# A feed-forward and Fourier-mixing kernel on one core: where ScalarE's long sums of magnitudes may stand among its copies out of PSUM

## The chip, the core and the metric

The kernel runs on one core of a Trainium2 chip. The metric is the device time of one execution in microseconds (us), the median of several runs. TensorE (PE in the profile) multiplies and writes PSUM. ScalarE (ACT) and VectorE (DVE) read PSUM, and every bank that PE fills must be copied or added out by one of them before PE may use it again. GpSimd (POOL) does a maximum across partitions and issues some DMAs. SyncE (SP) issues the others.

## What is computed

```python
x = A_x
xn = _layernorm(x, axis=-1)                      # 2048 x 576
a = einsum("bsd,ed->bse", xn, dft_hid_re)        # Fourier part
b = einsum("bsd,ed->bse", xn, dft_hid_im)
y = einsum("ts,bse->bte", dft_seq_re, a) - einsum("ts,bse->bte", dft_seq_im, b)
h = maximum(einsum("bsd,df->bsf", xn, w1), 0)    # w1: 576 x 4608
return x + y + einsum("bsf,fd->bsd", h, w2)      # w2: 4608 x 576
```

All of it is in float32. The kernel gives TensorE each float32 number as two float16 numbers, a high part and a low part (three products stand for one). For that each block of a weight matrix is first scaled by a power of two that is found from the sums of its magnitudes.

## The kernel before

**Steps.** The 4608 hidden columns are cut into nine blocks of 512 (b = 0 to 8), the 2048 rows into four groups of 512 (g = 0 to 3). A step is one (b, g). For b of 2 and more, 28 steps, both matrix products are done with seven half-size products in place of eight (Strassen's scheme as Winograd has it). This is the stage that the change is about. It starts at 213.6 us and ends at 821.3 us of the profiled span.

**The order of products in a step** is written out by hand (L925 to L932). A step makes the hidden values of its own (b, g) in two pairs of column tiles, `first` and `second`, and multiplies the hidden values of the step before it by w2 (`m`). With P1 and so on for the products of `first`, a prime for those of `second`, and m0 to m6 for the seven products of `mlp2`, PE's order is

P1 P2 m0 P6 P5 m1 P1' P7 m2 P2' P3 P4 m3 P6' m4 P5' m5 P7' m6 P3' P4'

P1, P6 and P7 have 6 matmuls of 256 columns, P2, P3, P4 and P5 have 8, each m has 12 of 288 columns.

**PSUM banks of the pairs** (`pair_products`, L418). P1, P6, P7 and P4 of one pair all add into one bank `u`; P2 has the bank `v`; P5 and then P3 have the bank `w`. Behind most products one instruction takes the bank's running content out (`free`, L465 to L472): ScalarE copies after P1 (L466), P6 (L468) and P5 (L469), VectorE adds after P2 (L467), P7 (L470) and P3 (L471). The next product on the same bank waits for it: P6 for the copy of P1, P7 for the copy of P6, P3 for the copy of P5, P4 for the add of P7. Later ScalarE and VectorE make the two float16 halves of the hidden values: relu copies (L447) with their remainders (L448), a relu on the sum r21 (L476), four sums (L451 to L454), their high half (`end_hi`, L459) and their low half (`end_lo`, L462).

**The seven products with w2** (`mlp2`, L496) go to two PSUM tiles. m0, m2, m3 and m6 are copied out by ScalarE (L519), m1, m4 and m5 are added by VectorE (L521); sums go to DRAM by accumulating DMAs from POOL's queue (`spill`, L523).

**Preparing the next block's weights.** `prepare_block(b + 1)` is a list of small jobs in `todo`; `work()` takes the next one, and a step calls it ten times (the `ready` places of the written order). The jobs are: load w1's two halves (L107), wait some places, sum of magnitudes of a half on ScalarE (`sum_w1`, L581, 1280 elements), power of two from it (POOL's maximum L121, small VectorE instructions), splits into high and low (ScalarE L182, VectorE L183) and sums of blocks (`sums_w1`, L593 to L597), then w2 the same way (load L100, `sum_w2` L610, 1152 elements, splits, `sums_w2` L640 to L643). The pool `raw` has two buffers for the unsplit weights, so a load can start only when the splits of the load two before it are done.

**Magnitudes of the Fourier matrices.** Between the products, `count` (L924) takes the next of 65 passes over them: `sum_c(m - 1)` sums the magnitudes of a tile of 128 x 1024 on ScalarE (L880), then `first_c(m)` loads the next tile (512 KB, L873) into the same single buffer. Every step takes two passes: one after P4, one after m6.

**What fixes the order on an engine.** When the program is built, each engine gets one fixed list. A job that is expected to be ready early may stand ahead of others that come before it in the program. `tc.issue_after(x)` forbids an instruction to stand ahead of x on x's engine. `order["s"]` is the latest `end_hi` (L459), `order["acc"]` the latest L521. `sum_c` may not stand ahead of `order["s"]`. `sum_w1` and `sum_w2` have no such bound.

Of the kernel before, what the change touches and what calls it, by code (L numbers as in the profile page):

```python
# [2 lines left out]

# [10 lines left out]
AF = mybir.ActivationFunctionType  # L14
# [35 lines left out]
def kernel(  # L50
# [364 lines left out]

    banks1, ends = [], []

    def pair_products(b, g, i):  # L418

        if not banks1:  # L420
            banks1.extend(ps1.tile([P, G], F32, tag="ps1", name=f"bank{k}")[:, :GH] for k in range(4))
        h = hs[b, g, i] = mlp.tile([P, 2, 7, GH], F16, tag="h", name=f"h{b}_{g}_{i}", bufs=4)
        st = mlp.tile([P, 5, GH], F32, tag="stage", name=f"s{b}_{g}_{i}")
        r21, s1, s2, s3, s4 = (st[:, n] for n in range(5))
        u, v, w = banks1[i], banks1[2], banks1[3]
        c11, c22 = cbufs[i], cbufs[2]
        tt, stt = nc.vector.tensor_tensor, nc.vector.scalar_tensor_tensor

        def product(n):
            ps = {P2: v, P5: w, P3: w}.get(n, u)  # L430
            first = n in (P1, P2, P5)
            x, ws, a = right(g, n), w1s[b, i], LEFT[n]
            todo = [
                (ws[:, y, a + k], x[z][:, k]) for k in range(2) for y, z in ((1, 0), (0, 0), (0, 1))
            ]
            if n in REST:
                k, c = REST[n]
                todo += [(ws[:, y, k], xT[g][:, KM, (H1, H2)[c]]) for y in range(2)]
            for m, (l, r) in enumerate(todo):
                nc.tensor.matmul(  # L440
                    ps, l, r, start=first and m == 0, stop=m == len(todo) - 1,
                    skip_group_check=not first,
                )

        def value(q, src):
            hi, lo = h[:, 0, q], h[:, 1, q]
            nc.scalar.activation(hi, src, AF.Relu)  # L447
            stt(lo, src, 0.0, hi, ALU.max, ALU.subtract)  # L448

        def end_s():  # L450
            stt(s3, c11, 0.0, r21, ALU.max, ALU.subtract)  # L451
            stt(s1, c22, 0.0, r21, ALU.max, ALU.add)
            stt(s2, c22, 0.0, s3, ALU.max, ALU.subtract)
            stt(s4, u, 0.0, s2, ALU.max, ALU.subtract)  # L454

        hi_s, lo_s = (h[:, k, S1 : S4 + 1] for k in range(2))

        def end_hi():
            order["s"] = nc.scalar.activation(hi_s, st[:, 1:], AF.Copy).ins  # L459

        def end_lo():
            order["lo"] = nc.vector.tensor_tensor(lo_s, st[:, 1:], hi_s, ALU.subtract).ins  # L462


        free = {  # L465
            P1: lambda: nc.scalar.activation(c11, u, AF.Copy),  # L466
            P2: lambda: tt(c11, v, c11, ALU.add),  # L467
            P6: lambda: nc.scalar.activation(s1, u, AF.Copy),  # L468
            P5: lambda: nc.scalar.activation(c22, w, AF.Copy),  # L469
            P7: lambda: tt(c22, u, c22, ALU.add),  # L470
            P3: lambda: tt(r21, w, s1, ALU.add),  # L471
        }  # L472
        use = {
            P2: lambda: value(A11, c11),
            P7: lambda: value(A22, c22),
            P3: lambda: nc.scalar.activation(r21, r21, AF.Relu),  # L476
            P4: lambda: (value(A12, u), end_s(), ends.extend((end_hi, end_lo))),
        }

        def run(n, used=False):  # L480
            if used:
                return use[n]()
            product(n)
            if n in free:
                free[n]()

        return run
# [8 lines left out]
    def mlp2(b, g, n):  # L496
# [19 lines left out]
        o = sums[row, col] = sums[row, col] if b else blocks[:, row, col]  # L516
        if b and n in (0, 2, 3, 6):
            o = sums[row, col] = sumbufs[next(turns) % len(sumbufs)]
            nc.scalar.activation(o, ps, AF.Copy, scale=us[b])  # L519
        else:  # L520
            order["acc"] = nc.vector.scalar_tensor_tensor(o, ps, us[b], o, ALU.mult, ALU.add).ins  # L521
        if b and n not in (0, 2, 3):
# [48 lines left out]
    def sum_w1(b, i):  # L571
# [6 lines left out]
        else:  # L578
            junk = w1bufs[b % 2 * 2 + i].bitcast(F16)
            w1s[b, i] = junk.rearrange("p (n k f) -> p n k f", n=2, f=P)  # L580
        nc.scalar.activation(  # L581
            junk[:, : 2 * KT * P].rearrange("p (k f) -> p k f", f=P), raws["w1", b, i], AF.Abs,
            scale=2.0**-10, accum_out=mx["w1", b][:, i : i + 1],
        )
        if b < BB:
            mx["b", i] = small.tile([P, 1], BF16, tag=f"mb{i}", name=f"mb{b}_{i}")
            nc.vector.tensor_copy(mx["b", i], mx["w1", b][:, i : i + 1])
# [11 lines left out]
    def sum_w2(b, i):  # L599
# [7 lines left out]
        else:  # L607
            new_w2(b, i)
            junk = w2s[b, i][:, 0, :4]
        nc.scalar.activation(  # L610
            junk, raws["w2", b, i], AF.Abs, scale=2.0**-10, accum_out=mx["w2", b][:, i : i + 1]
        )

    def power_w2(b):

# [32 lines left out]
    def split_w2(b, i, c):  # L648
# [4 lines left out]
        q = (slice(B11, B22 + 1), slice(T3, T1 + 1), slice(T4, T2 + 1))[c]  # L653
        split(w[:, 0, q], w[:, 1, q], src, sc["w2", b][:, i : i + 1])

    def prepare_w1(b, i):
        p = power_w1(b, i)
        if b < BB:
# [6 lines left out]
                lambda: split_w1(b, 2 * i + 1),  # L665
            ]
        return [
            lambda: (sum_w1(b, i), next(p)),
            lambda: None,
            lambda: later(p),  # L670
        ], [
# [6 lines left out]

    def prepare_w2(b):
        p = power_w2(b)  # L680
        steps = [
            lambda: sum_w2(b, 0),
            lambda: (sum_w2(b, 1), b > 1 and next(p)),
            lambda: later(p) if b else next(p, None),
        ]
        steps += [lambda i=i: (split_w2(b, i, 0), sums_w2(b, i)) for i in range(NQ)]
        for i in range(NQ):
            steps += [lambda: None] * 2
            steps += [lambda i=i, c=c: split_w2(b, i, c) for c in (1, 2)]
        return steps  # L690

    def prepare_block(b):

        wait = [lambda: None] * (2 if b < BB else 3)
        (m0, s0), (m1, s1) = prepare_w1(b, 0), prepare_w1(b, 1)
        return (
            [lambda: (load_w1(b, 0), load_w1(b, 1))] + wait
            + m0 + s0 + [lambda: load_w2(b, 0)] + m1 + s1 + [lambda: load_w2(b, 1)]
            + wait + prepare_w2(b)
        )  # L700


# [109 lines left out]
    steps = [(b, g) for b in range(NB) for g in range(NG)]  # L812
    todo = []

    def work():
        if todo:
            todo.pop(0)()

    dsp = None

# [54 lines left out]
    def sum_c(m):  # L875

        n, q = divmod(m, 4)
        f = firsts.pop(m)
        with tc.issue_after(order["s"]):
            nc.scalar.activation(  # L880
                f, f, AF.Abs, scale=2.0**-10, accum_out=sums_c[:, n, q : q + 1]
            )
# [5 lines left out]
    for n in range(2, len(steps)):  # L888
# [29 lines left out]
        if b >= BB:  # L918
# [2 lines left out]
            m = lambda q: mlp2(pb, pg, q)  # L921
            end = lambda q: ends and ends.pop(0)()
            ready = lambda q: [work() for _ in range(q)]
            count = lambda q: n > 3 and passes and passes.pop(0)()  # L924
            for do, q in (  # L925
                (first, P1), (first, P2), (m, 0), (end, 0), (first, P6), (ready, 1),
                (first, P5), (later1, P2), (ready, 1), (m, 1), (end, 0), (second, P1), (ready, 1),
                (first, P7), (m, 2), (second, P2), (ready, 1), (first, P3), (first, P4), (count, 0),
                (later1, P7), (m, 3), (second, P6), (later1, P3), (later1, P4), (later2, P2),
                (ready, 1), (m, 4), (second, P5), (ready, 1), (m, 5), (end, 0), (second, P7),  # L930
                (end, 0), (ready, 1), (m, 6), (count, 0), (ready, 2), (second, P3), (second, P4),
                (later2, P7), (later2, P3), (later2, P4), (ready, 1),  # L932
            ):
                do(q)
            for _ in range(4):
# [256 lines left out]
```

## Time and profile before

| | |
|---|---|
| median of 3 runs | 1275.6 us (1275.18 to 1277.2) |
| the profiled execution's own time | 1277.31 us |
| its span, first to last instruction | 1275.5 us |
| stage of the 28 steps | 213.6 to 821.3 us |
| granted TensorE clock | 0.999 |

A row of a timeline gives start, duration, engine, line, operation, out<-in, shapes and count; in brackets how long the engine sat idle before it and what ended that. A row of the waits gives engine and line, what it waited for, and then the idle us in total, how many times, the longest. A row of the windows gives the length of a stretch and each engine's busy us in it. `SPq` is SyncE's queue, where the instruction only issues a DMA; PEld is the weight load beside the matmuls. PE's ends are modelled: a row of 12 matmuls shows 1.63 us although the next product may begin 1.47 us after it.

### The profile page before, as it was taken

How to read it: one execution, taken by the hardware profiler on the slowest of the kernel's cores; microseconds unless marked ns; L12 is line 12 of the kernel's file. 1: busy time of each engine (PE TensorE's matmuls, PEld its weight loads, DVE VectorE, ACT ScalarE, POOL GpSimd, SP SyncE). 2: the span in 40 equal slices, each digit the busy share in tenths (PEclk: the TensorE clock that was granted, in tenths of full speed). 3: DMA queues.
4: the chain of work that ended last, by engine and by line, in shares of the span. 5: the costliest groups of instructions: out<-in, count | busy, mean ns of one | idle time of the engine just before them, and what ended most of it. 6: DMA issues, size and time to landing. Idle time of an engine off the chain costs nothing.

```text
span 1275.5 us, 25491 instructions
## 1 busy us (share of the span) xinstructions
PE 1242.4 (97%) x10396; PEld 987.9 (77%) x10396; DVE 998.6 (78%) x1875; ACT 730.1 (57%) x1222; POOL 149.2 (12%) x188
## 2 busy tenths in 40 slices
PE   8799999999999999999999999999999999999998
PEld 7565566888888878888888888877777777777776
DVE  8989997786887777777868877546788788878875
ACT  5846466676677676776766766534553333333332
POOL 2320011111112121211111111200000000000000
PEclk9999999999999999999999999999999999999999
DMA  6112457566766575665666665630043434434320
GB/s 244 43 66 66 133 123 151 131 115 146 143 129 126 134 146 126 128 144 120 121 145 142 132 136 120 122 96 1 1 161 104 146 116 153 129 117 143 121 85 20
DMA packets 60806, 150.75 MB, mean 118 GB/s; under 512 B 6288, under 2 KB 21136, under 8 KB 60688
## 3 DMA queue, kind: packets, MB, share of 16 engines
q1 hardware_dynamic: 42256, 111.36, 26.9%
q0 software_dynamic: 18432, 37.76, 20.9%
q8 instruction: 81, 1.33, 0.4%
q14 instruction: 37, 0.30, 0.1%
HBM read 101.91 MB, written 47.19 MB: 117 GB/s over the span
## 4 chain that ended last, share of the span: by engine, by line
PE 62%; DVE 20%; DMA 8%; ACT 6%; issue 4%; POOL 1%; SPq 0%; ACTq 0%; POOLq 0%; DVEq 0%
PE p L1126 23%; PE bank L440 15%; PE p L510 15%; PE pd L1008 7%; DMA raw_w<-in_w_dram 3%; DVE w2s L183 2%; DMA f<-in_cre_dram 1%; PE p L310 1%; DVE h L448 1%; ACT f L880 1%; DVE h L462 1%; ACT h L459 1%; DVE acc L521 1%; DMA spill<-sums 1%; DVE h L354 1%
## 5 line engine op out<-in xcount | busy, mean ns | idle before, releaser
L510 PE MATMUL p<-w2s,h 128*128 128x288 f16 x3024 | 409.7, 286 | 4.4 <-DVE acc L521 2.1
L510 PEld LDWEIGHTS <-h 128*128 128x128 f16 x3024 | 295.1, 98 | 81.5 <-issue 6.2
L1126 PE MATMUL p<-R,cs 128*128 128x288 f16 x2688 | 329.8, 286 | 1.7 <-DVE o L1132 1.7
L1126 PEld LDWEIGHTS <-cs 128*128 128x128 f16 x2688 | 263.0, 98 | 68.3 <-issue 2.0
L182 ACT ACTIVATE cs<-c,sc_c 128x1024 f16<-128x1024 f32 x112 | 128.4, 1148 | 193.2 <-PE p L1126 145.6
L440 PEld LDWEIGHTS <-w1buf 128*128 128x128 f16 x1600 | 156.5, 98 | 29.1 <-issue 8.1
L183 DVE SCALAR_TENSOR_TENSOR cs<-c,sc_c,cs 128x1024 f16<-128x1024 f32 x112 | 143.6, 1282 | 40.8 <-ACT cs L182 40.7
L440 PEld LDWEIGHTS <-dbuf 128*128 128x128 f16 x1200 | 117.4, 98 | 21.4 <-issue 5.8
L440 PE MATMUL bank<-xT,w1buf 128*128 128x256 f16 x832 | 109.9, 273 | 2.7 <-ACT acc L469 2.6
L462 DVE TENSOR_TENSOR h<-s,h 128x1024 f16<-128x1024 f32 x56 | 68.5, 1223 | 48.8 <-ACT h L459 48.8
L440 PE MATMUL bank<-acc,w1buf 128*128 128x256 f16 x768 | 102.1, 272 | 2.8 <-DVE acc L470 1.5
L1008 PE MATMUL pd<-dbuf,xT 128*128 128x288 f16 x832 | 104.1, 286 | 0.6 <-DVE R L1037 0.6
L1008 PEld LDWEIGHTS <-xT 128*128 128x128 f16 x832 | 80.7, 98 | 22.9 <-issue 2.9
L523 POOL DMA_DIRECT2D spill<-dbuf x74 | 64.3, 871 | 289.8 <-DVE dbuf L521 223.3
L440 PE MATMUL bank<-xT,dbuf 128*128 128x256 f16 x624 | 82.3, 273 | 1.4 <-ACT acc L469 1.4
L447 ACT ACTIVATE h<-acc 128x256 f16<-128x256 f32 x112 | 46.3, 414 | 58.8 <-DVE acc L470 42.5
L440 PE MATMUL bank<-acc,dbuf 128*128 128x256 f16 x576 | 76.6, 272 | 2.5 <-DVE acc L470 1.1
L1132 DVE SCALAR_TENSOR_TENSOR o<-p,us_c,o 128x288 f32<-128x288 f32 x112 | 57.4, 512 | 20.1 <-PE p L1126 19.5
L448 DVE SCALAR_TENSOR_TENSOR h<-acc,h 128x256 f16<-128x256 f32 x112 | 47.2, 421 | 32.0 <-ACT h L447 31.8
L459 ACT ACTIVATE h<-s 128x1024 f16<-128x1024 f32 x56 | 59.0, 1053 | 22.5 <-DVE s L454 21.3
L880 ACT ACTIVATE f<-f 128x1024 f32<-128x1024 f32 x64 | 67.2, 1050 | 5.4 <-DMA f<-in_cre_dram 5.4
L519 ACT ACTIVATE dbuf<-p,c_ub 128x576 f32<-128x576 f32 x74 | 54.2, 732 | 20.5 <-ACT h L447 11.3
(161 smaller groups left out, 1531.5 us busy)
## 6 DMA issues: line engine op xcount, KB each, us to landing
spill<-dbuf POOLq DMA_DIRECT2D x74, 288.0 KB, 5.1
f<-in_cre_dram SPq DMA_DIRECT2D x32, 512.0 KB, 4.3
f<-in_cim_dram SPq DMA_DIRECT2D x32, 512.0 KB, 3.8
c<-in_cre_dram SPq DMA_DIRECT2D x32, 512.0 KB, 4.5
c<-in_cim_dram SPq DMA_DIRECT2D x32, 512.0 KB, 4.8
spill<-sum POOLq DMA_DIRECT2D x38, 288.0 KB, 5.1
raw_w<-in_w_dram SPq DMA_DIRECT2D x17, 640.0 KB, 5.0
raw_w<-in_w_dram SPq DMA_DIRECT2D x18, 576.0 KB, 3.8
```

Of the source, the lines that this page charges most:

```text
L182: nc.scalar.activation(hi, src, AF.Copy, scale=s)
L183: nc.vector.scalar_tensor_tensor(lo, src, s, hi, ALU.mult, ALU.subtract)
L440: nc.tensor.matmul(ps, l, r, start=first and m == 0, stop=m == len(todo) - 1, skip_group_check=not first,)
L448: stt(lo, src, 0.0, hi, ALU.max, ALU.subtract)
L459: order["s"] = nc.scalar.activation(hi_s, st[:, 1:], AF.Copy).ins
L462: order["lo"] = nc.vector.tensor_tensor(lo_s, st[:, 1:], hi_s, ALU.subtract).ins
L510: nc.tensor.matmul(ps[:, c], h[:, x, qa, c * P : (c + 1) * P], w[:, y, qb], start=first and i == 0 and j == 0, stop=i == NQ - 1 and j == 2 ...
L523: nc.gpsimd.dma_start(spill[g, row, col], o, accum_op=ALU.add)
L880: nc.scalar.activation(f, f, AF.Abs, scale=2.0**-10, accum_out=sums_c[:, n, q : q + 1])
L1008: nc.tensor.matmul(ps[j], xT[g][:, kx, c * P : (c + 1) * P], dsp[j][:, hl, k], start=(t % 2 == 0 and n == 0), stop=(t % 2 == 1 and n == le ...
L1126: nc.tensor.matmul(ps, w[:, a, k], r[:, c, rq], start=first and k == 0 and j == 0, stop=k == HK - 1 and j == 2, skip_group_check=not first,)
L1132: nc.vector.scalar_tensor_tensor(o, ps, us["c"][:, n : n + 1], o, ALU.mult, ALU.add)
```

## The change

Four things are changed. `order["free"]` now holds the latest ScalarE copy out of PSUM (L466, L468, L469, L519), and every long sum on ScalarE may not stand ahead of it (w1's from block 3 on, w2's from block 2 on, and `sum_c`). The sums of w1 and w2 are marked `long`, and seven of the ten places are `brief` (the three that stay `ready` are those before m1, behind P1' and behind P2'): there a long job is not taken but owed, and the next `ready` place takes one job more. The first `count` of a step moves from behind P4 to behind P5'. The empty places among the jobs are redistributed: five in place of three before w1's first sum, one in place of three before w2's, one more between w2's two sums, one fewer before each half's last splits.

```diff
+    def freed(i):
+        order["free"] = i.ins
...
-            P1: lambda: nc.scalar.activation(c11, u, AF.Copy),
+            P1: lambda: freed(nc.scalar.activation(c11, u, AF.Copy)),
-            P6: lambda: nc.scalar.activation(s1, u, AF.Copy),
-            P5: lambda: nc.scalar.activation(c22, w, AF.Copy),
+            P6: lambda: freed(nc.scalar.activation(s1, u, AF.Copy)),
+            P5: lambda: freed(nc.scalar.activation(c22, w, AF.Copy)),
...
-            nc.scalar.activation(o, ps, AF.Copy, scale=us[b])
+            freed(nc.scalar.activation(o, ps, AF.Copy, scale=us[b]))
...
+        with tc.issue_after(order["free" if b > BB else "s"]):
             nc.scalar.activation(
                 junk[:, : 2 * KT * P].rearrange("p (k f) -> p k f", f=P), raws["w1", b, i], AF.Abs,
...
+        with tc.issue_after(order["free"]) if b >= BB else nullcontext():
             nc.scalar.activation(
                 junk, raws["w2", b, i], AF.Abs, scale=2.0**-10, accum_out=mx["w2", b][:, i : i + 1]
...
+    def long(f):
+        f.long = True
+        return f
...
-            lambda: (sum_w1(b, i), next(p)),
+            long(lambda: (sum_w1(b, i), next(p))),
...
-            lambda: sum_w2(b, 0),
-            lambda: (sum_w2(b, 1), b > 1 and next(p)),
+        steps = [long(lambda: sum_w2(b, 0))] + [lambda: None] * (b >= BB)
+        steps += [
+            long(lambda: (sum_w2(b, 1), b > 1 and next(p))),
...
-            steps += [lambda: None] * 2
+            steps += [lambda: None] * (1 if b >= BB else 2)
...
-        wait = [lambda: None] * (2 if b < BB else 3)
+        wait, wait2 = ([lambda: None] * n for n in ((2, 2) if b < BB else (5, 1)))
...
-    def work():
-        if todo:
-            todo.pop(0)()
+    owed = []
+    def work(short=False):
+        if not todo:
+            return
+        if short and getattr(todo[0], "long", False):
+            owed.append(1)
+            return
+        todo.pop(0)()
+        if not short and owed:
+            owed.pop()
+            work(True)
...
-        with tc.issue_after(order["s"]):
+        with tc.issue_after(order.get("free", order["s"])):
             nc.scalar.activation(
                 f, f, AF.Abs, scale=2.0**-10, accum_out=sums_c[:, n, q : q + 1]
...
+            brief = lambda q: [work(True) for _ in range(q)]
...
-                (first, P1), (first, P2), (m, 0), (end, 0), (first, P6), (ready, 1),
+                (first, P1), (first, P2), (m, 0), (end, 0), (first, P6), (brief, 1),
                 (first, P5), (later1, P2), (ready, 1), (m, 1), (end, 0), (second, P1), (ready, 1),
-                (first, P7), (m, 2), (second, P2), (ready, 1), (first, P3), (first, P4), (count, 0),
+                (first, P7), (m, 2), (second, P2), (ready, 1), (first, P3), (first, P4),
                 (later1, P7), (m, 3), (second, P6), (later1, P3), (later1, P4), (later2, P2),
-                (ready, 1), (m, 4), (second, P5), (ready, 1), (m, 5), (end, 0), (second, P7),
-                (end, 0), (ready, 1), (m, 6), (count, 0), (ready, 2), (second, P3), (second, P4),
-                (later2, P7), (later2, P3), (later2, P4), (ready, 1),
+                (brief, 1), (m, 4), (second, P5), (count, 0), (brief, 1), (m, 5), (end, 0), (second, P7),
+                (end, 0), (brief, 1), (m, 6), (count, 0), (brief, 2), (second, P3), (second, P4),
+                (later2, P7), (later2, P3), (later2, P4), (brief, 1),
```

## The prediction

> **What bounds the kernel.** I read in this order: the page's busy times, the windows of single steps, PE's waits in the stage of the 28 steps, and the timelines of one long and one clean step.
>
> ```profile
> PE 1242.4 (97%) x10396; PEld 987.9 (77%) x10396; DVE 998.6 (78%) x1875; ACT 730.1 (57%) x1222; POOL 149.2 (12%) x188
> ...
> 213.60:821.30 607.70, 598.20 (x5155) 503.95 (x5153) 457.06 (x1002) 417.90 (x808) 106.63 (x134) 1.00 0.63 133
> ...
> 387.24:408.45 21.21, 21.21 (x187) 18.00 (x184) 13.89 (x31) 14.31 (x30) 4.25 (x6) 1.00 0.62 130
> 408.45:429.66 21.21, 21.21 (x187) 18.01 (x185) 16.89 (x39) 14.21 (x28) 3.03 (x4) 1.00 0.61 132
> 429.66:450.86 21.20, 21.20 (x186) 18.00 (x184) 15.86 (x40) 15.46 (x31) 4.35 (x6) 1.00 0.66 136
> 450.86:474.06 23.20, 21.84 (x187) 17.97 (x185) 19.17 (x40) 16.97 (x32) 3.32 (x5) 1.00 0.62 131
> 474.06:496.45 22.39, 21.36 (x186) 17.99 (x184) 13.87 (x31) 14.30 (x30) 4.28 (x6) 1.00 0.62 124
> ```
>
> PE is busy 97% of the span, so only its waits can be won. A window row has length, then busy PE, PEld, DVE, ACT, POOL. Steps (4,0) to (4,2) take 21.21 us with PE never idle; (4,3) takes 2.00 more and (5,0) 1.19 more. 28 clean steps would be 28 x 21.21 = 593.9 us; the stage takes 607.7. So 13.8 us is the ceiling of any gain here.
>
> ```profile
> PE bank L440 <- ACT acc L469: 3.9, 5, 0.9
> PE bank L440 <- DVE acc L470: 2.6, 7, 0.4
> PE bank L440 <- ACT s L468: 1.0, 1, 1.0
> ```
>
> The largest wait is for ScalarE's copy of P5 (L469), five times. This is how one comes about, at the end of (4,3):
>
> ```profile
> 468.50 1.27 ACT L581 ACTIVATE w1buf<-raw_w 128x1280 f16<-128x1280 f32 x1 [2.67 <-DMA raw_w<-in_w_dram]
> 469.66 1.63 PE L510 MATMUL p<-w2s,h 128*128 128x288 f16 x12
> 469.77 1.04 ACT L459 ACTIVATE h<-s 128x1024 f16<-128x1024 f32 x1
> 470.72 1.04 ACT L880 ACTIVATE f<-f 128x1024 f32<-128x1024 f32 x1
> 471.76 0.36 ACT L469 ACTIVATE acc<-bank 128x256 f32<-128x256 f32 x1
> 472.17 1.03 PE L440 MATMUL bank<-xT,w1buf 128*128 128x256 f16 x8 [0.88 <-ACT acc L469]
> 473.19 0.81 PE L440 MATMUL bank<-acc,w1buf 128*128 128x256 f16 x6
> ```
>
> w1's sum (L581) stands in ScalarE's list before the copy of P5' and waits 2.67 us for its load. Then come the sum, a 1.04 us high half, a 1.04 us sum of the Fourier tile, and only then the copy that P3' waits for. The clean end of a step, and the start of the next:
>
> ```profile
> 514.44 1.63 PE L510 MATMUL p<-w2s,h 128*128 128x288 f16 x12
> 515.91 1.04 PE L440 MATMUL bank<-xT,dbuf 128*128 128x256 f16 x8
> 516.79 0.82 PE L440 MATMUL bank<-acc,dbuf 128*128 128x256 f16 x6
> 518.90 0.40 ACT L476 ACTIVATE s<-s 128x256 f32<-128x256 f32 x1
> 519.19 1.63 PE L510 MATMUL p<-w2s,h 128*128 128x288 f16 x12
> 519.20 0.36 ACT L447 ACTIVATE h<-bank 128x256 f16<-128x256 f32 x1
> 519.47 0.37 ACT L466 ACTIVATE acc<-bank 128x256 f32<-128x256 f32 x1
> 520.66 0.60 PE L440 MATMUL bank<-acc,dbuf 128*128 128x256 f16 x4
> ```
>
> m6 to P3' is 1.47, P3' to P4' 0.88: 0.109 a matmul of 256 columns. P1 and P2 (14 matmuls, 1.53) end at m0, so this step began at 517.66, and P6 starts 3.00 after a step's start. I use these offsets below.
>
> **The change part by part.** The sum is made against the profiled execution's 1277.31 us (span 1275.5 and 1.8 around it), which is 1.7 above the median of the runs shown, 1275.6.
>
> *1. w1's sums bound to the latest copy.* I counted the jobs through the places: the first half's sum now comes behind the copy of P5 in step (b,1), a whole step after its load, the second half's in (b,2). P1' is the next product that ScalarE copies, m1 and P1' later (1.47 + 0.65 = 2.1 us), longer than the sum (1.27 and its 0.19 of reading), and P6' needs that copy only six products on. Cost 0. If this cover went, P1' would be copied up to 1.5 us late, still ahead of P6'. What goes is the wait above: m6 to P3' was 2.51 against 1.47, then P3' to P4' 1.02 against 0.88, in all 1.18 with 0.88 of it idle in the row. The five waits have 3.9 idle, so 3.9 x 1.18 / 0.88 = **-5.2 us**.
>
> *2. The other long step, (5,0).*
>
> ```profile
> ACT sum L519 <- DMA spill<-sum: 2.3, 1, 2.3
> ```
>
> Its 1.19 us is the wait for L468 in PE's list. ScalarE was held by a copy that waited 2.3 us for an accumulating DMA, right behind the traffic of (4,3)'s end. Between 0 and -1.2; I take the middle, **-0.6**, because the transfers, not the sum, decide it.
>
> *3. The two passes over the Fourier matrices.* The work stays (64 sums, 64 loads), but pass one moves behind the copy of P5' and pass two is bound behind the copy of m6. Before, both were bound only to `end_hi`:
>
> ```profile
> 511.45 0.82 PE L440 MATMUL bank<-acc,dbuf 128*128 128x256 f16 x6
> 511.60 1.05 ACT L880 ACTIVATE f<-f 128x1024 f32<-128x1024 f32 x1
> 512.32 1.63 PE L510 MATMUL p<-w2s,h 128*128 128x288 f16 x12
> 512.76 0.33 SPq L873 DMA_DIRECT2D f<-in_cre_dram  x1
> ```
>
> P5' starts 15.00 us into the step (511.45 - 496.45) and ends at 15.87. Its copy starts 0.2 later and holds ScalarE for 0.3, so the sum of pass one starts at 16.3. The next load is issued 1.16 after a sum's start (511.60 to 512.76): 17.5. m6 ends at 19.46 and its copy at about 20.3. There pass two's sum stands, 2.8 us after its own load was issued.
>
> ```profile
> DMA to landing us min/median/max: 3.5/4.0/8.4
> ...
> DMA to landing us min/median/max: 5.4/5.4/5.4
> ```
>
> The first row is all loads of L873. So ScalarE will wait there in every step: an undisturbed load lands at 21.1 to 21.5. Behind this sum stand the relu on r21, the relu of P4' and the copy of P1, which P6 of the next step needs at 21.21 + 3.00 = 24.21. From the sum's start to the next ScalarE instruction is 1.04 (470.72 to 471.76), then 0.30 and 0.27 (518.90, 519.20, 519.47) and the copy's 0.37: 2.0 us. An undisturbed load costs nothing: 21.5 + 0.1 + 2.0 = 23.6, with 0.6 to spare. That cover is the three products P3' P4' P1 and P2 with m0.
>
> It is gone when another load runs beside. The second row of the fence is the one load issued at 503.89:
>
> ```profile
> 494.29 0.81 ACT L182 ACTIVATE w1buf<-raw_w,c_sw 128x640 f16<-128x640 f32 x1
> ...
> 503.20 0.33 SPq L100 DMA_DIRECT2D raw_w<-in_w_dram  x1
> 503.89 0.33 SPq L873 DMA_DIRECT2D f<-in_cim_dram  x1
> ```
>
> w2's load (L100) starts when the last split of a w1 half is done, 8.9 us after the first split (494.29 to 503.20). In the new order the first split comes about 8.0 us into steps (b,1) and (b,2): P5 ends at 4.53, then copy, sum, maximum, scale (an estimate from the durations above, with 1.6 us for maximum and scale). 8.0 + 8.9 = 16.9, just ahead of the Fourier load at 17.5, as in these rows. Then it lands after 5.4, at 22.9, and the copy of P1 is done at 22.9 + 0.1 + 2.0 = 25.0, 0.8 late. P6 waits; behind the sum the r21 chain is late as well, which m2 needs only at 28.5. That is two steps in each of six blocks: 12 x 0.8 = **+9.6 us**. Bounds: 0, if the list puts the copy of P1 ahead of the sum or the load lands in time; 12 x 1.4 = 16.8, if pass one's sum comes 0.6 later behind a split.
>
> Does the list really put the sum ahead of a copy that could go first? It did so before:
>
> ```profile
> 217.81 6.38 SPq L873 DMA_DIRECT2D f<-in_cre_dram  x2
> ...
> 222.68 1.06 ACT L880 ACTIVATE f<-f 128x1024 f32<-128x1024 f32 x1 [3.30 <-DMA f<-in_cre_dram]
> ```
>
> This sum stood first for 3.30 us while its load was under way. The list counts on earlier landings than the chip gives, as with L581.
>
> A rule of the Trainium skill speaks against this edit: DMA: Bandwidth & Descriptors, section "Rules for kernel authors", says to issue a DMA early and wait on its semaphore late. By it the halved distance between load and sum is a loss. The same page, section "Anatomy of one DMA — SWDGE (gpsimd) path", has a fit of 2.0 us plus bytes at 436 KB a us for another way of issue; as an estimate, 512 KB would land after 3.2 us and this term would be 0, the first rival below. The trace's shortest is 3.5 us and its loaded one 5.4, so the trace does not agree with the fit.
>
> *4. w2's sums and splits later.* Before, w2's sums stood at the end of (b,2), and the splits ran through the first 16 us of (b,3):
>
> ```profile
> 450.74 1.02 ACT L182 ACTIVATE w2s<-raw_w,c_sw 128x864 f16<-128x864 f32 x1 [0.68 <-DVE c_sw L632]
> ...
> 466.19 0.81 DVE L183 SCALAR_TENSOR_TENSOR w2s<-raw_w,c_sw,w2s 128x576 f16<-128x576 f32 x1
> ```
>
> Now the sums come behind the copies of P5 and P1' in (b,3), and the splits start some 11 us later, running into (b+1,0). DVE has 19.17 us of work in (4,3) against 13.87 in (5,0). The crowded stretch cost (4,3) 2.00 - 1.18 = 0.82, mostly P4 behind L470. In its new place it meets P4' behind L470', whose slack is m6 and P3' (2.35 us) in place of m2, P2' and P3 (3.2 us). Bounds: 6 x -0.82 = -4.9 if nothing waits any more; if every wait grows by the 0.85 of lost slack, 6 x 0.85 = +5.1. DVE's load splits over two steps, which helps; the slack is smaller, which hurts. I take **+0.6**.
>
> *5. The rest.* `sum_w2`'s own durations, the empty places, the places of block 1 and the last block's order lie beside a busy PE: 0.
>
> Sum: -5.2 - 0.6 + 9.6 + 0.6 = +4.4 us; 1277.31 + 4.4 = 1281.7 for a profiled execution, less 1.7: **1280.0 us**.
>
> **The rivals.** *Sums that never reach PE* (faster): pass two's sum is followed by the copy of P1 in time, because the list has r21's relu, P4''s relu or that copy ahead of it, or the loads land 0.8 us earlier. For it: undisturbed loads have 0.6 us of slack; w2's load may start after the Fourier load. Against: the rows at 217.81 and 503.20. Then -5.2 - 0.6 + 0.6 = -5.2: 1270.4. It decides at a landing 22.1 us into the step.
>
> *Half of it*: the copy of P1 is late in 12 steps by 0.4 only. -5.8 + 4.8 + 0.6 = -0.4: 1275.2, no change that a measurement can tell.
>
> *The crowded stretch takes over* (slower): P4' waits the full 0.85 more in six steps, and with late splits ahead of the copy of P1 also 0.5 there: 6 x 1.35 = 8.1 in place of 0.6, so 1287.5. For it: DVE's 19.17 us. Against: its work now lies over two steps.
>
> That the change doesn't do what it says: the second sum of w2 stands two products before a copy, m2's, not more; but m2's copy is needed five products later, so this costs nothing and changes no case.
>
> **How the numbers follow.** Late load 0.42, sums that never reach PE 0.36, half of it 0.13, crowded stretch 0.09. The likeliest is the first, 1280.0, with a range of its own of 1277 to 1286. 0.2% is 2.6 us, about what can be told from no change. Faster 0.36, same 0.14, slower 0.50. The range that leaves out 2 in 10 goes from 1267, a little under the faster rival (w2's waits half gone), to 1288.
>
> **What would show it.** Right: L581 never waits for raw_w, PE's five waits for L469 are gone, (b,3) ends without them; L880 waits for DMA some 25 times, about 1 us each; PE waits for L466 at P6 of (b,2) and (b,3), 12 times, about 0.8 us. Wrong: L880 after m6 but no wait of PE for L466; L880 waiting for nothing; or PE's waits for L470 gone from (b,3) without a like wait at P4'.

## The result, and the profile after

The changed kernel takes 1358.31 us (1356.73 to 1361.7, 5 runs) against 1275.6 us for the kernel before in the same session: a ratio of 1.065, 95% interval 1.0631 to 1.0668. It is 82.7 us slower. The prediction was 1280.0, with a range up to 1288. All profiles below number lines as the changed kernel or the experiment does: L444 is the pairs' matmul, L514 the matmul with w2, L470, L472 and L473 ScalarE's copies after P1, P6 and P5, L474 and L475 VectorE's adds after P7 and P3 (L475 makes r21), L480 the relu on r21, L463 `end_hi`, L455 to L458 the four sums ahead of it, L523 ScalarE's copies and L525 VectorE's adds out of the banks of `mlp2`, L527 their accumulating DMA, L182 and L183 the splits, L646 to L649 w2's sums of blocks, L901 the passes' sum, L894 its load.

From the page of the changed kernel (its profiled execution took 1361.7 us): the busy times, the group of the passes' sums with its idle time, and three rows of DMA landings.

```profile
PE 1263.2 (93%) x10396; PEld 994.6 (73%) x10396; DVE 999.0 (73%) x1875; ACT 726.3 (53%) x1222; POOL 147.7 (11%) x188
...
L901 ACT ACTIVATE f<-f 128x1024 f32<-128x1024 f32 x64 | 67.3, 1051 | 88.9 <-DMA f<-in_cre_dram 47.0
...
spill<-dbuf POOLq DMA_DIRECT2D x74, 288.0 KB, 6.9
f<-in_cre_dram SPq DMA_DIRECT2D x32, 512.0 KB, 5.1
f<-in_cim_dram SPq DMA_DIRECT2D x32, 512.0 KB, 5.1
```

The 64 sums are as long as before (67.3 us in all), but ScalarE now stands idle for 88.9 us in front of them. PE is busy for 1263.2 us instead of 1242.4 with the same 10396 instructions, so its matmuls themselves have become longer somewhere. The windows of the four steps (5,0) to (5,3), and of the whole stage, in the columns of the windows before:

```profile
509.36:532.45 23.09, 21.74 (x186) 17.82 (x184) 13.36 (x27) 11.83 (x24) 3.47 (x5) 1.00 0.64 154
532.45:554.57 22.12, 21.53 (x186) 17.98 (x184) 16.19 (x37) 15.12 (x30) 3.30 (x5) 1.00 0.52 108
554.57:581.27 26.70, 22.95 (x187) 18.74 (x184) 16.74 (x38) 15.35 (x31) 4.32 (x6) 0.94 0.55 118
581.27:609.70 28.43, 23.16 (x187) 18.71 (x185) 19.13 (x45) 18.04 (x34) 3.85 (x6) 0.94 0.50 94
212.77:904.24 691.47, 621.19 (x5154) 511.64 (x5152) 456.27 (x1002) 414.85 (x807) 106.12 (x135) 0.97 0.54 115
```

The stage of the 28 steps grew from 607.70 to 691.47 us, by 83.8: all of the loss is here. It has two parts. PE's idle time went from 607.70 - 598.20 = 9.5 to 691.47 - 621.19 = 70.3 us (+60.8), and PE's busy time for the same matmuls by 621.19 - 598.20 = 23.0 us. The steps (b,2) and (b,3) carry most of it, 5.5 and 7.2 us more than the clean 21.21, and just there the granted clock (third number from the right) is 0.94 instead of 1.00.

What PE and ScalarE wait for in the stage, first PE, then ScalarE:

```profile
PE bank L444 <- ACT acc L470: 46.1, 20, 4.5
PE bank L444 <- DVE s L475: 13.3, 6, 2.7
```

```profile
ACT f L901 <- DMA f<-in_cre_dram: 47.0, 14, 5.6
...
ACT f L901 <- DMA f<-in_cim_dram: 39.4, 13, 5.1
```

27 of the sums wait for their load, 3.2 us each on average; PE waits 20 times for the copy of P1 that stands behind such a sum, and six times, once in each (b,3), for the r21 add. The waits for the copy of P5 are gone. This is how a wait for the copy of P1 comes about, at the end of step (5,1), which begins at 532.45 (timeline of the changed kernel):

```profile
548.12 0.82 PE L444 MATMUL bank<-acc,dbuf 128*128 128x256 f16 x6
...
549.95 1.06 ACT L463 ACTIVATE h<-s 128x1024 f16<-128x1024 f32 x1 [0.83 <-DVE s L458]
...
550.65 0.33 SPq L100 DMA_DIRECT2D raw_w<-in_w_dram  x1
550.92 0.36 ACT L473 ACTIVATE acc<-bank 128x256 f32<-128x256 f32 x1
551.18 1.05 ACT L901 ACTIVATE f<-f 128x1024 f32<-128x1024 f32 x1
...
551.61 0.86 POOL L527 DMA_DIRECT2D spill<-sum  x1 [8.91 <-DVE sum L525]
...
552.34 0.33 SPq L894 DMA_DIRECT2D f<-in_cim_dram  x1
...
553.46 0.86 POOL L527 DMA_DIRECT2D spill<-dbuf  x1 [0.99 <-DVE dbuf L525]
...
554.87 0.86 POOL L527 DMA_DIRECT2D spill<-dbuf  x1 [0.55 <-ACT dbuf L523]
...
559.44 1.06 ACT L901 ACTIVATE f<-f 128x1024 f32<-128x1024 f32 x1 [4.87 <-DMA f<-in_cim_dram]
...
561.07 0.37 ACT L470 ACTIVATE acc<-bank 128x256 f32<-128x256 f32 x1
...
561.49 2.72 PE L444 MATMUL bank<-acc,dbuf 128*128 128x256 f16 x12 [3.75 <-ACT acc L470]
```

Read it from the top. P5' is issued from 548.12 on. Its copy (L473) runs only at 550.92, because `end_hi` (L463) stands ahead of it in ScalarE's list and waits for a VectorE sum. The first pass follows at 551.18 and its load goes out at 552.34, 19.9 us into the step, 1.7 us behind w2's load (L100) and with three accumulating transfers (L527) issued around it. The second pass is ready to run and waits 4.87 us, to 559.44, for this load, 7.1 us after its issue. Behind it the copy of P1 ends at 561.44, and P6, whose place in a clean step is 3.00 us after the step's start, so 557.57, starts at 561.49. Then its matmuls and the next product's come 12 in 2.72 us, 0.22 apart instead of the 0.109 of a clean step: after this idle time TensorE runs at half its rate.

### The profile page after: what moved, and what is told of

Its sections match the earlier page's. It is cut to its first block, busy times and chain, and to the rows that moved or that the text cites. A ratio compares the mean times of both kernels' runs of the same rounds, so it can differ in the third digit from the quotient of the medians.

```text
span 1359.9 us, 25517 instructions
## 1 busy us (share of the span) xinstructions
PE 1263.2 (93%) x10396; PEld 994.6 (73%) x10396; DVE 999.0 (73%) x1875; ACT 726.3 (53%) x1222; POOL 147.7 (11%) x188
## 4 chain that ended last, share of the span: by engine, by line
PE 51%; DVE 17%; DMA 13%; ACT 12%; issue 5%; POOL 1%; SPq 0%; ACTq 0%; POOLq 0%; DVEq 0%
PE p L1148 23%; PE p L514 9%; PE pd L1030 8%; PE bank L444 7%; DMA f<-in_cre_dram 6%; DMA f<-in_cim_dram 5%; ACT f L901 4%; PE p L310 3%; DVE h L452 1%; DVE dbuf L183 1%; ACT h L463 1%; DVE w1buf L183 1%; DVE w2s L183 1%; ACT acc L473 1%; DVE h L466 1%
## 5 line engine op out<-in xcount | busy, mean ns | idle before, releaser
L514 PE MATMUL p<-w2s,h 128*128 128x288 f16 x3024 | 420.6, 290 | 13.3 <-DVE h L466 3.2
L514 PEld LDWEIGHTS <-h 128*128 128x128 f16 x3024 | 298.1, 99 | 99.3 <-issue 11.2
L182 ACT ACTIVATE cs<-c,sc_c 128x1024 f16<-128x1024 f32 x112 | 128.4, 1148 | 194.1 <-PE p L1148 150.4
L444 PEld LDWEIGHTS <-w1buf 128*128 128x128 f16 x1600 | 158.8, 99 | 59.4 <-issue 36.1
L183 DVE SCALAR_TENSOR_TENSOR cs<-c,sc_c,cs 128x1024 f16<-128x1024 f32 x112 | 143.6, 1283 | 42.1 <-ACT cs L182 41.9
L444 PEld LDWEIGHTS <-dbuf 128*128 128x128 f16 x1200 | 119.6, 100 | 51.4 <-issue 33.5
L444 PE MATMUL bank<-acc,w1buf 128*128 128x256 f16 x768 | 106.8, 281 | 31.8 <-ACT acc L470 23.5
L901 ACT ACTIVATE f<-f 128x1024 f32<-128x1024 f32 x64 | 67.3, 1051 | 88.9 <-DMA f<-in_cre_dram 47.0
L444 PE MATMUL bank<-xT,w1buf 128*128 128x256 f16 x832 | 110.7, 274 | 0.8 <-DVE s L458 0.8
L455 DVE SCALAR_TENSOR_TENSOR s<-acc,s 128x256 f32<-128x256 f32 x56 | 23.7, 422 | 115.8 <-ACT s L480 115.8
L444 PE MATMUL bank<-acc,dbuf 128*128 128x256 f16 x576 | 80.9, 283 | 29.6 <-ACT acc L470 22.5
L527 POOL DMA_DIRECT2D spill<-dbuf x74 | 64.1, 866 | 296.8 <-DVE dbuf L525 271.5
L451 ACT ACTIVATE h<-acc 128x256 f16<-128x256 f32 x112 | 46.1, 412 | 82.4 <-DVE acc L471 43.6
L466 DVE TENSOR_TENSOR h<-s,h 128x1024 f16<-128x1024 f32 x56 | 68.5, 1223 | 23.6 <-ACT h L463 23.6
L444 PE MATMUL bank<-xT,dbuf 128*128 128x256 f16 x624 | 83.6, 275 | 1.3 <-DVE s L458 1.3
L1154 DVE SCALAR_TENSOR_TENSOR o<-p,us_c,o 128x288 f32<-128x288 f32 x112 | 57.5, 513 | 20.1 <-PE p L1148 19.9
L463 ACT ACTIVATE h<-s 128x1024 f16<-128x1024 f32 x56 | 59.1, 1056 | 15.3 <-DVE s L458 14.4
```

The costliest lines, as they stand in the source:

```text
L182: nc.scalar.activation(hi, src, AF.Copy, scale=s)
L183: nc.vector.scalar_tensor_tensor(lo, src, s, hi, ALU.mult, ALU.subtract)
L444: nc.tensor.matmul(ps, l, r, start=first and m == 0, stop=m == len(todo) - 1, skip_group_check=not first,)
L514: nc.tensor.matmul(ps[:, c], h[:, x, qa, c * P : (c + 1) * P], w[:, y, qb], start=first and i == 0 and j == 0, stop=i == NQ - 1 and j == 2 ...
L527: nc.gpsimd.dma_start(spill[g, row, col], o, accum_op=ALU.add)
L901: nc.scalar.activation(f, f, AF.Abs, scale=2.0**-10, accum_out=sums_c[:, n, q : q + 1])
```

## The experiments

All compare with the kernel before on the same chip, 1276.4 to 1277.5 us there.

| run | what it is | us | ratio, interval |
|---|---|---|---|
| e1 | changed, first pass back behind P4 | 1274.27 | 0.9973, 0.9963 to 0.9983 |
| e2 | before, with the passes' edits alone | 1339.07 | 1.0479, 1.0428 to 1.053 |
| e3 | changed, without the loads | 1275.93 | 0.999, 0.9978 to 1.0002 |
| e4 | before, with the bounds of w1's and w2's sums alone | 1272.86 | 0.9965, 0.9951 to 0.9978 |
| e5 | before, with the first pass's place alone | 1276.71 | 0.9994, 0.9983 to 1.0006 |
| e6 | before, with the passes' bound alone | 1272.63 | 0.9967, 0.9958 to 0.9977 |
| e7 | changed, half of each load | 1332.58 | 1.0437, 1.0414 to 1.046 |
| e8 | before, with all bounds | 1273.04 | 0.9969, 0.9957 to 0.998 |
| e9 | changed, second pass behind the next m1 | 1307.05 | 1.0224, 1.0188 to 1.0261 |
| e10 | passes as in e9, weights as before | 1285.38 | 1.0063, 1.0047 to 1.0078 |
| e11 | all bounds and the first pass's place | 1335.83 | 1.0458, 1.0432 to 1.0483 |
| e12 | changed, one job place later | 1355.24 | 1.0615, 1.0597 to 1.0632 |

The theories on trial first: A, the second pass stands too close behind its own load; B, the moved weight jobs crowd ScalarE and VectorE. **Which half of the change does it?**

```diff
-                (first, P7), (m, 2), (second, P2), (ready, 1), (first, P3), (first, P4),
+                (first, P7), (m, 2), (second, P2), (ready, 1), (first, P3), (first, P4), (count, 0),
...
-                (brief, 1), (m, 4), (second, P5), (count, 0), (brief, 1), (m, 5), (end, 0), (second, P7),
+                (brief, 1), (m, 4), (second, P5), (brief, 1), (m, 5), (end, 0), (second, P7),
```

> The changed kernel, but the first of the two passes over the Fourier matrices is back behind P4; every bound and every job of the weights stays as changed. Theory A (the second pass's sum stands 2.8 us behind its own load and holds ScalarE until it lands, so the copy of P1 and then P6 are late): PE's waits for L470 go, from 46 us to under 3, and with them the slow clock; what stays is P5' behind L475 in (b,3), about 13 us and its echo, so 1280 to 1295 us. Theory B (the moved jobs of the weights are what costs): stays above 1340 us.

The passes' edits alone, on the kernel before:

```diff
-        with tc.issue_after(order["s"]):
+        with tc.issue_after(order.get("free", order["s"])):
...
-                (first, P7), (m, 2), (second, P2), (ready, 1), (first, P3), (first, P4), (count, 0),
+                (first, P7), (m, 2), (second, P2), (ready, 1), (first, P3), (first, P4),
...
-                (ready, 1), (m, 4), (second, P5), (ready, 1), (m, 5), (end, 0), (second, P7),
+                (ready, 1), (m, 4), (second, P5), (count, 0), (ready, 1), (m, 5), (end, 0), (second, P7),
```

> The kernel before, with only the two edits on the passes: the first moved behind P5', both sums bound behind the latest copy out of PSUM. The jobs of the weights are as before. Theory A: most of the loss is here alone, 1310 to 1350 us, L880's line waits for its DMA in nearly every step. Theory B: within 6 us of 1275.6.

One place undone brings 84 us back and leaves the kernel a little faster than before; the passes' edits alone cost 62. e1 is faster than was expected: the waits for r21, which were to stay, are gone as well. PE's waits in e2 are those of the changed kernel without the ones for r21:

```profile
PE bank L444 <- ACT acc L470: 54.9, 27, 5.4
```

**Is it the sum's place on ScalarE, or its load?** e3 keeps the changed kernel's whole order and loads only the first of the 64 tiles.

```diff
         n, q = divmod(m, 4)
-        f = firsts[m] = mlp.tile([P, HK, P], F32, tag="first", name=f"f{n}_{q}", bufs=1)
+        if m:
+            firsts[m] = firsts["kept"]
+            return
+        f = firsts[m] = firsts["kept"] = mlp.tile([P, HK, P], F32, tag="first", name=f"f{n}_{q}", bufs=1)
```

> The changed kernel, but only the first of the 64 loads of Fourier tiles in the passes is done; each pass sums that tile again, with scale 1 in place of 2^-10, so the scales of the Fourier part are not the reference's and 63 loads of 512 KB are left out. ScalarE's instructions and their order of issue bounds are the same. Theory A (the load is what is late, not the 1.24 us of the sum in that place): PE's waits for L470 under 2 us, 1275 to 1295 us. Theory B: above 1340 us. A third way, that the sum's own time in that place is what makes the copy of P1 late: above 1300 us with waits for L470.

```profile
PE bank L444 <- DVE s L475: 8.1, 6, 1.4
...
PE bank L444 <- ACT acc L470: 0.3, 1, 0.3
```

All 64 sums run, 1.05 us each, where the change puts them, and 46.1 us of waiting for the copy of P1 are 0.3. So the sums' length and place cost nothing by themselves: the late load does. The waits for r21 stay, at 1.35 us each instead of 2.2, so the moved jobs cost next to nothing where no load runs beside them.

**The bounds of the weights' sums alone** (e4: `issue_after(order["free"])` around `sum_w1` and `sum_w2` as in the change's diff, nothing else of it).

> The kernel before, with only the bounds on the sums of w1 and w2 (not ahead of the latest copy out of PSUM); places, passes and their bound as before. Theory A with the first term of the prediction: the five waits for L469 at the end of (b,3) go, 1268 to 1272 us. Theory B: no gain or slower, 1275 us or more.

```profile
PE bank L444 <- ACT s L472: 2.8, 7, 0.8
...
PE bank L444 <- ACT acc L473: 0.5, 1, 0.5
```

The waits for the copy of P5 went from 3.9 us in five to 0.5 in one; those for the copy of P6 grew from 1.0 us in one to 2.8 in seven. The median fell by 4.5 us, a little less than expected. In the traces the stage, from the first to the last matmul of the pairs, is 2.9 us shorter (214.6 to 819.3 in place of 213.6 to 821.2). So the first term of the sum is there, but not all of the 4.5 us need belong to it.

**Place or bound?** e5 has only the place of the first `count` changed (the second and third hunk of e2's diff), e6 only the bound (its first hunk).

> The kernel before, with only the place of the first pass moved from behind P4 to behind P5' (the bound stays the last end_hi copy). Theory A (late load): what counts is how much of ScalarE's work lies between a pass's own load and its next sum. The bound to end_hi lets both sums stand where they stood, some ten ScalarE instructions apart, so this costs nothing: 1274 to 1281 us, no wait of a sum for a DMA over 1 us. Rival P (the place alone does it, because the load is issued later): 1320 to 1345 us, as the two edits together had.

> The kernel before, with only the bound of the passes' sums changed to the last copy that frees PSUM; the passes stay behind P4 and behind m6. Theory A: the sums stand eleven to sixteen ScalarE instructions apart, 7 us and more, so a load of 5 to 8 us is nearly always there: 1272 to 1281 us, waits of the sums for DMA under 10 us in total. Rival B (the bound alone does it): 1320 to 1345 us.

Neither costs anything; e6 is even 0.33% faster. The waits for the copy of P5 are gone in e6 too, although its weights' sums have no bound, so they do not need e4's bound to go. With the old bound, the list lets the sum stand at its old position wherever the program has it: e5's order on ScalarE around the sums is that of before, with nine or more instructions between a first sum and the second nearly everywhere. With the old place, the bound leaves ten or eleven between them (e6). Only place and bound together leave few: four or two in e2, two in the changed kernel and five in (b,3). The load of the second sum is issued when the first is done. In e6 these loads land after 5.0 and 5.6 us in the median, no sooner than in the changed kernel, and no sum waits for one: what counts is the distance.

**Does the landing follow the load's bytes?**

```diff
-        f = firsts[m] = mlp.tile([P, HK, P], F32, tag="first", name=f"f{n}_{q}", bufs=1)
-        nc.sync.dma_start(f, blocks_c(n)[q])
+        if not m:
+            firsts["kept"] = mlp.tile([P, HK, P], F32, tag="first", name=f"f{n}_{q}", bufs=1)
+        f = firsts[m] = firsts["kept"]
+        k = HK if not m else HK // 2
+        nc.sync.dma_start(f[:, :k], blocks_c(n)[q][:, :k])
```

> The changed kernel, but every load of the Fourier part after the first brings only half of the tile (256 KB instead of 512 KB; the sum still runs over the whole tile, so the scales of that part differ). Theory A with the landing growing with its bytes: loads land in 2.8 to 4.5 us instead of 5.1 to 7.8, the second sum waits 0.5 to 2.5 us less than before in each step, the waits of P6 fall from 46 us to 5 to 20, TensorE's idle times stay under 3.5 us so that its slow stretches vanish: 1285 to 1315 us. Rival D (the landing is set by a fixed delay or by the queue, not by bytes): landing median stays above 4.8 us and the time above 1340 us.

The landings (page of e7) and the waits for the copy of P1:

```profile
f<-in_cim_dram SPq DMA_DIRECT2D x32, 256.0 KB, 4.2
f<-in_cre_dram SPq DMA_DIRECT2D x31, 256.0 KB, 4.4
```

```profile
PE bank L444 <- ACT acc L470: 30.8, 16, 3.0
```

Both expectations of the time missed. Half the bytes save only 0.7 to 0.9 us of 5.1, and the time falls by 25.7 us, 0.92 us for each of the 28 steps. So the chain holds (what the load gains, the step gains), but most of a landing here isn't its own bytes. The Trainium skill, page "DMA: Bandwidth & Descriptors", section "Queues, rings and completion order", says that a DMA engine takes turns between the queues that have work for it, packet by packet. e10's rows below agree in that other transfers stretch with it; no run here shows the turns themselves.

**Spread the two passes.** e9 leaves the first behind P5' and puts the second behind the next step's m1; e10 does the same on the kernel before with the passes' bound, without the weights' edits.

```diff
-                (first, P5), (later1, P2), (ready, 1), (m, 1), (end, 0), (second, P1), (ready, 1),
+                (first, P5), (later1, P2), (ready, 1), (m, 1), (count, 0), (end, 0), (second, P1), (ready, 1),
...
-                (end, 0), (brief, 1), (m, 6), (count, 0), (brief, 2), (second, P3), (second, P4),
+                (end, 0), (brief, 1), (m, 6), (brief, 2), (second, P3), (second, P4),
```

> The changed kernel with the first pass left behind P5' and the second moved from behind m6 to behind m1 of the next step. Everything else as changed. Theory A: load and sum are eleven ScalarE instructions apart, 7 us or more, so nearly nothing waits: 1270 to 1282 us, waits of the sums for DMA under 12 us in total (the loads beside the weights' load, 6.4 to 7.8 us, are the ones that may still be late). Rival E (a long sum right behind the copy of P5' is itself late for P1's copy, whatever the load does): P1's copy late by about 1 us in 24 steps, 1295 to 1310 us.

> The kernel before with the passes' bound, the first pass behind P5' as in the change, and the second behind m1 of the next step; the weights' sums and jobs as before. Theory A: of the 30 us that the same spread left with all of the change, nearly all lies in (b,3), where the moved w2 jobs stand ahead of the r21 add. With w2 as before it is gone: 1272 to 1283 us, and no wait of PE for that add over 1 us. Rival S (the first load, issued just then, holds up the partial outputs' transfers and so their buffers): 1290 to 1307 us whatever w2 does, with ScalarE waiting 30 us or more for those transfers.

e9's time falls into rival E's range, yet not for its reason: no wait for the copy of P1 is left. Its waits, and one of them at the start of (5,3):

```profile
PE bank L444 <- DVE s L475: 15.5, 6, 2.6
PE bank L444 <- ACT s L472: 8.1, 8, 1.7
```

```profile
557.50 0.74 ACT L523 ACTIVATE sum<-p,c_ub 128x576 f32<-128x576 f32 x1 [3.12 <-DMA spill<-sum]
...
558.56 0.81 PE L444 MATMUL bank<-acc,dbuf 128*128 128x256 f16 x6 [1.30 <-ACT s L472]
```

e10 tells the two apart: without the weights' edits 21.7 us go, with them the r21 waits (0.9 us are left), and 8 us over the kernel before remain. These are ScalarE's waits for accumulating transfers, first e10's waits, then the landings on the pages of e10, e6 and e3:

```profile
ACT dbuf L523 <- DMA spill<-dbuf: 15.5, 13, 2.5
...
ACT sum L523 <- DMA spill<-sum: 12.4, 8, 2.9
```

```profile
spill<-dbuf POOLq DMA_DIRECT2D x74, 288.0 KB, 6.4
```

```profile
spill<-dbuf POOLq DMA_DIRECT2D x74, 288.0 KB, 4.6
```

```profile
spill<-dbuf POOLq DMA_DIRECT2D x74, 288.0 KB, 4.7
```

e6 has the same bound and the same 64 loads, at other moments, and its transfers land as fast as with no loads at all (e3). A load that goes out behind P5' runs into the partial outputs and stretches them to 6.4 us. Both theories were partly right: neither 1283 at most nor 1290 at least.

**The bounds together, and the weights' moves.** e8 adds the bounds of e4 and e6; e11 adds the first pass's place to e8, so it is the change without its moved jobs.

> The kernel before with all of the change's new bounds (sums of the passes, of w1 and of w2) and none of its moves. Theory A: each bound alone gave 4 to 5 us, mostly from the same few waits of PE for the copy of P5; sums and loads stay eleven or more ScalarE instructions apart, so nothing is late: 1268 to 1274 us. Rival: two bounds push each other's sums ahead of P1's copy, 1276 to 1290 us.

> The changed kernel without its second idea: all bounds and the first pass behind P5', but the places of the w1 and w2 jobs as before (no brief, no longer waits ahead of the w2 splits). Theory A: the late second load costs what it cost with the passes' edits alone, and the 19 us between that run and the full change come from the moved w2 jobs: 1330 to 1345 us. Rival B (the sums' bounds cost the 19 us): 1350 to 1362 us.

The two gains don't add up: e4, e6 and e8 all stand at 0.997, and so does e1. No version here is better than that. e11's 1335.83 puts the moved jobs at 22.5 us of the change's 82.7; e9 against e10 gave 21.7. Both pairs have the loads behind P5'. Without loads (e3), and with the pass behind P4 (e1), the same moved jobs cost nothing, so this price needs both.

**Why do they cost that?** In (5,3) of the changed kernel four pairs of w2's block sums and two splits stand ahead of the r21 add on VectorE, and P5' waits:

```profile
598.92 0.82 DVE L646 TENSOR_TENSOR raw_w<-raw_w 128x288 f32<-128x288 f32 x2
...
601.87 0.42 DVE L475 TENSOR_TENSOR s<-bank,s 128x256 f32<-128x256 f32 x1
...
602.34 1.44 PE L444 MATMUL bank<-acc,dbuf 128*128 128x256 f16 x6 [2.60 <-DVE s L475]
```

In e1, with the same moved jobs but the pass behind P4, the add stands ahead of them all, and this wait doesn't occur:

```profile
547.09 0.42 DVE L475 TENSOR_TENSOR s<-bank,s 128x256 f32<-128x256 f32 x1
...
548.06 2.15 DVE L183 SCALAR_TENSOR_TENSOR w2s<-raw_w,c_sw,w2s 128x864 f16<-128x864 f32 x2 [0.54 <-ACT w2s L182]
...
550.12 0.82 DVE L646 TENSOR_TENSOR raw_w<-raw_w 128x288 f32<-128x288 f32 x2
```

e12 moves the place of these jobs behind the products that fill r21:

```diff
-                (first, P7), (m, 2), (second, P2), (ready, 1), (first, P3), (first, P4),
+                (first, P7), (m, 2), (second, P2), (first, P3), (first, P4), (ready, 1),
```

> The changed kernel with one place for a weight job moved from behind P2' to behind P4. Theory L: in (b,3) both first splits of w2 with their eight sums of blocks (L646 to L649) stand ahead of the r21 add (L475) in VectorE's list, and the product P5' waits for that add; behind P4 the add stands ahead of them. Then the six waits for L475 (13.3 us) and the slow matmuls behind them go, some 15 to 22 us: 1332 to 1345 us, with the waits for the copy of P1 as before. Rival (VectorE has too much work in (b,3), whatever its order): the time stays above 1350 us and another wait of 10 us or more stands in (b,3).

```profile
PE bank L444 <- ACT acc L470: 46.5, 26, 4.2
PE bank L444 <- ACT acc L473: 9.2, 6, 2.1
```

My theory missed. The waits for the add are gone, but six waits for the copy of P5 took their place, and the median is only 3 us lower; the intervals of the two ratios (1.0597 to 1.0632 and 1.0631 to 1.0668) touch. The rival, too much work in (b,3) whatever its order, had the time right and its wait nearly: 10 us or more were expected, 9.2 stand there. The list still puts one split of w2 ahead of the add (none in e1, two and eight block sums in the changed kernel). This is one of the six new waits:

```profile
597.09 2.21 ACT L182 ACTIVATE w2s<-raw_w,c_sw 128x576 f16<-128x576 f32 x3
...
599.08 0.42 DVE L457 SCALAR_TENSOR_TENSOR s<-acc,s 128x256 f32<-128x256 f32 x1
...
599.61 0.38 ACT L473 ACTIVATE acc<-bank 128x256 f32<-128x256 f32 x1 [0.31 <-DVE s L457]
...
600.05 0.27 PE L444 MATMUL bank<-xT,dbuf 128*128 128x256 f16 x1 [1.93 <-ACT acc L473]
```

Three splits of w2 stand ahead of the copy on ScalarE, and for its last 0.31 us it waits for L457, which now stands behind the eight block sums on VectorE. So the order of the add alone isn't enough; whether the order of the rest of (b,3) or the amount of work there decides is left open.

## Why the prediction was wrong

Its direction and its main mechanism were right: the second pass waits for its own load, the copy of P1 stands behind it, P6 is late, in (b,2) and (b,3) above all. The step that failed is the size of the third term, +9.6 us for "12 x 0.8", with an upper bound of 16.8. The twelve waits at P6 of (b,2) and (b,3) are all in PE's timeline, but they take 40.8 us, 3.4 each in place of 0.8. The sums wait for their load 27 times, as forecast ("some 25 times"), but 3.2 us each in place of about 1.

*The late load.* The working had the load issued 17.5 us into the step and landing 5.4 later, at 22.9. In (5,1) it is issued at 19.9 and read at 27.0, so P6 is not 0.8 but 561.49 - 557.57 = 3.9 us late (0.9 of the 22.12 us of that step were lost earlier in it). Two statements gave this. "Its copy starts 0.2 later" took the copy of P5' from a list in which the sum stood first; in the new list `end_hi` comes ahead, waits for VectorE, and the copy starts 1.9 us after P5' has ended. And 5.4 was the landing of a load that went out beside w2's load and one accumulating transfer, for which POOL had been idle 7.64 us (trace of before):

```profile
504.53 0.86 POOL L523 DMA_DIRECT2D spill<-dbuf  x1 [7.64 <-DVE dbuf L521]
```

At the new moment there are three, and it lands after 7.0. That these three stretch it is likely, but no run changes them alone. The bound of 16.8 allowed for neither: it took the landing as given while moving the load to another moment.

*The clock.* The sum priced idle time alone. The trace before held no idle time of PE over 1.0 us in the stage, so a rate that depends on it could not be read there; 23.0 of the 83.8 us are matmuls that became longer.

*w2's later jobs* were to cost +0.6 and at most 5.1; they cost about 22 beside the passes. The waits for L474 in (b,3) did go, as "what would show it" allowed, but the next wait was not P4' behind L474 (the prediction's L470'): it was P5' behind the r21 add, a wait that the working had not listed, with the half clock behind it. In e1 the same moved jobs are free, and in e3, without the loads, too, so the price belongs to the two edits and the loads together, and a sum of parts could not show it.

*w1's bound* was right in kind: -5.2 forecast, all five waits gone in the changed kernel. By itself no run has it: e4, with w2's bound as well, is 4.5 us faster, 2.9 of it seen in the stage. *The step (5,0)* did not gain its 0.6: it takes 23.09 us.

*The bounds of the range.* The rival with a crowded stretch had 1287.5. No case let the two costs and the clock come together.

## What to carry to other kernels

Before moving a consumer, count the instructions of its engine between it and the issue of its own load, in the list and not in the program: two edits that were free alone (0.9994 and 0.9967) brought the instructions in between from nine and more to four or two, at 62 us. A load's landing belongs to the moment of its issue (5.4 us in the row of before, 7.0 here); when the issue moves, take the landing from rows with the same transfers beside it, and look for the transfers that it will stretch in turn. Where a matmul engine is 97% busy, price an idle time of some microseconds at more than itself.

## What the runs showed of the hardware

In the stage of the changed kernel TensorE's granted clock is either whole or half. By the trace's record of it, it is half in eleven stretches, ten of 3.41 us and one of 6.83, which start at whole multiples of 3.41 us from one another; before, the stage has none. An estimate: 41.0 us at half the rate cost 20.5 us, most of the 23.0 by which the matmuls became longer.

The stretches come with idle time. After 3.75 us idle, 12 matmuls of 256 columns took 2.72 us, 0.22 apart, against 0.109 in a clean step, and the granted clock of the steps (b,2) and (b,3) of block 5 reads 0.94. After the 1.30 us in e9 six took 0.81 us as always. This bears out the Trainium skill, page "TensorE: Matmul & The Clock Gate", section "Part 1: The HAM clock gate (the "warmup" mystery)", by which about 3.4 us without work put the clock at half. But here the length alone doesn't decide: after 3.50 us idle (262.89 in the changed kernel) 12 matmuls took 1.47 us as always, and after 2.07 us (509.25 in e2) they took 2.67. The six waits for r21 in e9 are 2.58 us each; behind four of them the clock is half, behind two it stays whole. One of each, in the columns of the windows (the clock is the third number from the right):

```profile
389.70:393.00 3.30, 3.30 (x29) 2.77 (x29) 3.30 (x9) 2.72 (x7) 0.69 (x1) 1.00 0.01 2
...
571.90:575.30 3.40, 3.40 (x18) 2.26 (x16) 3.40 (x8) 2.62 (x5) 0.89 (x1) 0.50 0.09 14
```

That it matters where an idle time falls on the 3.41 us fits both, but is not tested here.

A 512 KB load landed after 3.6 us at its fastest, 5.1 in the median and 7.8 at its slowest in the stage of the changed kernel. Half the bytes (e7) brought the median down by 0.7 to 0.9 us only, so most of the landing is not the load's own bytes; what ran beside it is the likely rest:

```profile
DMA to landing us min/median/max: 3.6/5.1/7.8
```
